# Attention with a gate: Q of the second half in seven block products, weights read back as stored parts

## The chip, the cores and the metric

The kernel runs on one core of a Trainium2 chip. The metric is the device time of one execution in microseconds. A core has TensorE (PE: matrix products into PSUM), VectorE (DVE), ScalarE (ACT), GpSimd (POOL) and SyncE (SP), which here only issues transfers; 16 DMA engines move data between DRAM and SBUF.

## What is computed

```python
def _A_ref(x, k_cache, v_cache, wq, wo):          # x: 1 x 2048 x 640, 32 heads of 128
    W = min(4096, max(256, Sk // 4))              # 512 keys, the last of 2048
    q = (x @ wq).reshape(B, Sq, Hq, Dh)           # by head
    scores = einsum("bhqd,bhkd->bhqk", q, k[last W]) * Dh ** -0.5
    p = softmax(scores)
    o = einsum("bhqk,bhkd->bhqd", p, v[last W])
    return o.reshape(B, Sq, Hq * Dh) @ wo
def _B_ref(x, w1, b1, w2, b2):
    return relu(x @ w1 + b1) ** 2 @ w2 + b2       # 640 -> 1728 -> 640
xn = layernorm(x)
return x + _A_ref(xn, ...) * silu(_B_ref(xn, ...))
```

## The kernel before

**Precision.** Each matrix product of float32 values is made of parts: an operand is split into a high part (a copy to float32r on ScalarE) and a low part (the value less its high part, on GpSimd or VectorE). `triple` issues three products, high·high, high·low and low·high, into one PSUM bank. One such product, 128 x 128 weights against 512 columns, is called a pass below.

**Stages.** The normalised x is transposed and split tile by tile (four tiles of 512 rows, `xT_d[t][i]` in DRAM, i = 0 high, 1 low). The dense branch B comes first; for its two middle tiles it already uses block products with seven multiplications (`w_first` to `w_third`). Then come 128 attention units.

**Units.** A unit is one head against one tile of 512 query rows. There are two halves (hf = 0: tiles 0 and 1; hf = 1: tiles 2 and 3), in each 16 groups of two heads (`G` = 2), in a group two tiles by two heads: four units (`UPG`). The last unit of the first half and the first of the second meet at the seam, unit 64. In a unit i TensorE makes:

- `s_mm`: scores of the unit, four banks s, 12 passes;
- `q_mm`: Q of unit i + 2 (`AHEAD`), bank pq, five blocks of D, 15 passes;
- `v_mm`: P·V of unit i - 1, bank o, 12 passes;
- `r_mm`: output products of a finished pair of heads, banks r, five blocks d in two units, 15 passes a unit on average.

The other engines work behind them. VectorE folds each score bank to a maximum (`max_fold`, tile rdm), ScalarE gathers it to 32 partitions (`gather`), VectorE ends it (`row`, rowm). SP stores that row to DRAM (m_d) and reads it back as a broadcast over 128 partitions (bm). VectorE subtracts it from the scores (`shift`, tile e), ScalarE takes the exponential (`expo`) and the high part of P (`p_hi`, pt), GpSimd the two low parts (`p_lo`) and between them the sum of the halves (`s_add`, su). The sum goes the same way over `s_fold`, `gather`, `row` (s_d) and a broadcast bs, with which VectorE scales o (`o_norm`); ScalarE and VectorE split it (`o_hi`, `o_lo`, ot), and `r_acc` adds each r to the accumulator acc.

Weights (`load_raw`, `prep`): in both halves the raw K, V, output and Q weights of each head are loaded (kr, vr, or, qr) and split into wk, wv, wo, wq.

**Order.** Nothing is scheduled by a tool: `at(when, f, ...)` collects calls with a planned time, sorted at the end, and each engine takes its instructions in that order. `PERIOD` = 12.4 is the planned length of a unit. `pe.addr_align` (rows ISA) pads TensorE's instruction stream so that units start at fixed slots.

Of the kernel before, what the change touches and what calls it, by code (L numbers as in the profile page):

```python
# [20 lines left out]
SLOTS = (0, 11, 22, 33, 42)  # L21
LEAD_SLOT, MID_SLOT, LEAD_PADS, LEAD_STEPS = 76, 101, 5, range(4, 21)
# [3 lines left out]
def kernel(  # L26
# [64 lines left out]
    s_d = [dpool.tile([P, DC, NT], F32, name=f"s_d{t}") for t in range(NTILE // 2)]  # L91
    h_d = {f: dpool.tile([P, NT], F32, name=f"h_d{f}") for f in range(FC - 4, FC)}
# [20 lines left out]
    W_HOME = {}  # L113

    def home(f, k):

        n = chunks[f][1]
        if (f, k) not in W_HOME:
            if k:
                w = [pc.tile([P, D], F32R, tag=f"w2{i}", name=f"w2s{f}_{i}", bufs=3) for i in range(2)]  # L120
            elif n < P:
                w = [xp.tile([P, DC, 2 * n], F32R, tag="w1h", name=f"w1s{f}", bufs=1)]
            elif f < FA:
                w = [
                    pa.tile([P, DC, n], F32R, tag=f"w1{i}", name=f"w1s{f}_{i}", bufs=3)
                    for i in range(2)
                ]
            else:
                two = keep.tile([P, 2, D], F32R, tag="ot", name=f"w1s{f}", bufs=4)
                w = [two[:, i, :].rearrange("p (c n) -> p c n", n=n) for i in range(2)]  # L130
# [258 lines left out]
    def split_hi(f, r, k):  # L389
        act.activation(split_parts(f, k)[0], r, AF.Copy)  # L390

    def split_lo(f, r, k, engine):
        hi, lo = split_parts(f, k)
        engine.tensor_tensor(lo, r, raw(hi), op=ALU.subtract)
# [454 lines left out]
    def pair(tag, shape, name, bufs):  # L849
        return [  # L850
            pools["eo" if tag == "wo" else "ep"].tile(shape, F32R, tag=f"{tag}{i}", name=f"{name}_{i}", bufs=bufs)
            for i in range(2)
        ]

    def load_raw(kind, hf, h):
        r = raw_tile(kind, f"{kind}r{hf}_{h}")
# [6 lines left out]
    def prep(kind, hf, h, eng=None):  # L863
        shape = {"q": [P, DC, DH], "k": [P, W], "v": [P, KC, DH], "o": [P, D]}[kind]
        home = {"q": WQ, "k": KT, "v": VV, "o": WO}[kind]
        hi, lo = home[hf, h] = pair(f"w{kind}", shape, f"w{kind}{hf}_{h}", 2 * G if kind == "o" else G)
        src = RAW.pop((kind, hf, h))
        act.activation(hi, src, AF.Copy)
        (eng or pool).tensor_tensor(lo, src, raw(hi), op=ALU.subtract)

# [89 lines left out]
    def s_add(i):  # L960
        RD[i, "su"] = ap.tile([P, 2, NT], F32, tag="su", name=f"su{i}", bufs=1)
        pool.tensor_tensor(RD[i, "su"], E[i, 0], E[i, 1], op=ALU.add)

    def s_fold(i):
# [3 lines left out]
            RD.pop((i, "su")).rearrange("p c (b i) -> p c b i", i=B32),  # L968
# [24 lines left out]
    def o_hi(i):  # L993
        two = keep.tile([P, 2, D], F32R, tag="ot", name=f"ot{i}", bufs=2 * G)
        OT[i] = [two[:, k, :NT] for k in range(2)]
# [5 lines left out]
    def r_mm(i, d, js, k):  # L1001
        hf, g, t, h = units[i]
        if 0 in js:
            PRS[i, d] = bank(f"r{i}_{d}", k)
        for j in js:
# [3 lines left out]
                tuple(x[:, d * P : (d + 1) * P] for x in w),  # L1009
# [21 lines left out]
    def load_finish(n, hf, t, d):  # L1031
        t0 = (hf * TPH + t) * NT
        FX[n, hf, t, d] = tile = raw_tile(n, f"f{n}{hf}_{t}_{d}")
# [24 lines left out]
    def late_load(kind, f):  # L1058
        f0, n = chunks[f]
        if f % 2 == 0 or kind == 1 and f == 3:  # L1060
            r = raw_tile("q" if kind == 1 else "o", f"l{kind}r{f}")
        elif kind == 1 and f == 1:
            r = raw_tile("o", f"l{kind}r{f}")
        else:
            tag, bufs = ("su", 1) if kind == 1 else ("e", 3)
            r = ap.tile([P, 2, NT], F32, tag=tag, name=f"l{kind}r{f}", bufs=bufs)
# [9 lines left out]
    def late_prep(kind, f):  # L1076
# [8 lines left out]
        else:  # L1085
            hi, lo = LW[kind, f] = pair("wo", [P, D], f"l2w{f}", 2 * G)
# [52 lines left out]
    def late_h():  # L1139
        LR["h"] = pools["ep"].tile([P, DC, NT], F32, tag="x1", name="lh", bufs=TPH)  # L1140
        for f in range(FA, FC):
            sp.dma_start(LR["h"][:, f - FA, :], h_d[f])

    def late_hs(f):
        two = ap.tile([P, 2, NT], F32R, tag=f"pt{f % 2}", name=f"lh{f}", bufs=3)
        hi, lo = LH[f] = [two[:, k, :] for k in range(2)]
        r = LR["h"][:, f - FA, :]
# [18 lines left out]
    def late_split(f):  # L1166
        n = chunks[f][1]
        r = LR.pop(f)
        kind, bufs = ("wk", G) if f % 2 else ("q", AHEAD + 1)
        if n < P:  # L1170
            h = pools["ep"].tile([P, NT], F32R, tag=f"{kind}0", name=f"lh{f}", bufs=bufs)
            LH[f] = (h, h)
            hi, lo = h[:n, :], h[n : 2 * n, :]
        else:
            hi, lo = LH[f] = pair(kind, [P, NT], f"lh{f}", bufs)
# [20 lines left out]
    def late_x():  # L1196
        LR["x"] = pools["ep"].tile([P, DC, NT], F32, tag="x0", name="lx", bufs=TPH)
        for d in range(DC):
            sp.dma_start(LR["x"][:, d, :], xT[d * P : (d + 1) * P, LATE * NT : (LATE + 1) * NT])

    def late_gate(d):
# [6 lines left out]
        for j in js:  # L1208
            dve.tensor_tensor(a[:, j], sg[:, j], a[:, j], op=ALU.mult)
            dve.tensor_tensor(a[:, j], a[:, j], LR["x"][:, d, j], op=ALU.add)  # L1210
# [64 lines left out]
    for m in range(2 * FC):  # L1275
# [44 lines left out]
    gate(  # L1320
        T2,
        lambda d: pools["ep"].tile([P, NT], F32, tag=f"wv{d % 2}", name=f"sgl{d}", bufs=G),
    )
# [6 lines left out]
    pools["eo"] = ctx.enter_context(tc.tile_pool(name="eo", bufs=1, side="right"))  # L1330
    ap = ctx.enter_context(tc.tile_pool(name="at", bufs=2))
# [10 lines left out]

    for n in range(HALF * NG):
        hf, g = divmod(n, NG)
        base = UPG * PERIOD * n
        for j in range(G):
            h = g * G + j
            for kind, when in (
                ("q", (j - 1 - AHEAD) * PERIOD + (8.42 if j else 8.35)),
                ("k", (j - 2) * PERIOD + (8.5 if j else 8.37)),  # L1350
                ("v", j * PERIOD + 8.4),
                ("o", (j if n == 0 else -j) * PERIOD + 8.45),
# [228 lines left out]
```

## Time and profile before

| | |
|---|---|
| median of 3 runs | 1956.58 us (1956.53 to 1957.04) |
| profiled execution | 1955.08 us, span 1953.3 us |
| granted TensorE clock | 0.999 |
| TensorE, VectorE, ScalarE, GpSimd busy | 99%, 82%, 64%, 69% of the span |
| matrix products | 8576 |
| Q blocks of attention | from 296.93 us on |

A row of the chain or of a timeline has the start in us, the length in us, the engine, the source line (here always a helper's), the operation, out<-in by the tiles' names, and in brackets the idle time ahead of it and who ended it. A row of groups has count, busy us, mean ns, and idle time with who ended it. Tile names without numbers stand for all units.

### The profile page before, as it was taken

The numbers are of one execution on the slowest core, as the hardware profiler recorded it, in microseconds if no ns is written. First come the engines' busy times: TensorE is split into PE (matmuls) and PEld (weight loads), VectorE is DVE, ScalarE is ACT, GpSimd is POOL, SyncE is SP. The second block draws the span as 40 slices with busy tenths as digits, with TensorE's granted clock in tenths as the row PEclk, the third lists the DMA queues.
The fourth block names the chain that finished last, engine by engine and source line by source line (L and its number), as shares of the span: only waits on it lengthen the run. The fifth ranks groups of instructions, "written<-read, shape, count | busy, mean of one in ns | idle before, by whom it ended". The sixth has DMA issues, their size and how long they took to land.

```text
span 1953.3 us, 28587 instructions
## 1 busy us (share of the span) xinstructions
PE 1943.1 (99%) x8576; PEld 1605.8 (82%) x8576; DVE 1599.5 (82%) x2758; ACT 1242.6 (64%) x2150; POOL 1348.2 (69%) x729
## 2 busy tenths in 40 slices
PE   9999999999999999999999999999999999999998
PEld 7888878888888888888888888888888888888887
DVE  6864747788888888888888878888888888888864
ACT  5665536766666666666666676666666666666643
POOL 1022106888888888888888888888888888888841
PEclk9999999999999999999999999999999999999999
DMA  7557953333332233333335433443343333323253
GB/s 267 150 179 252 365 176 112 98 93 92 93 92 93 92 93 92 93 93 92 92 98 179 144 110 109 114 114 114 114 114 114 114 114 114 98 92 93 85 186 119
DMA packets 147639, 246.43 MB, mean 126 GB/s; under 512 B 25020, under 2 KB 47334, under 8 KB 146214
## 3 DMA queue, kind: packets, MB, share of 16 engines
q1 hardware_dynamic: 144486, 230.02, 38.6%
q0 software_dynamic: 2864, 14.42, 1.8%
q8 instruction: 77, 1.26, 0.2%
q14 instruction: 68, 0.56, 0.1%
q10 hardware_dynamic: 144, 0.16, 0.0%
HBM read 213.59 MB, written 30.95 MB: 125 GB/s over the span
## 4 chain that ended last, share of the span: by engine, by line
PE 97%; DMA 2%; DVE 0%; issue 0%; ACT 0%; SPq 0%; ACTq 0%; POOLq 0%; DVEq 0%
PE r L77 22%; PE pq L77 22%; PE s L77 18%; PE o L77 18%; PE py L77 6%; PE ph L77 2%; PE ly L77 2%; PE wa L77 2%; PE lu L77 2%; PE wy L77 1%; PE wx L77 1%; DMA w1r<-in_w_dram 1%; DMA ch<-h_m 1%; PE eu L77 1%; DMA xb<-in_x_dram 0%; DMA w2r<-in_w_dram 0%
## 5 line engine op out<-in xcount | busy, mean ns | idle before, releaser
L77 POOL TENSOR_TENSOR pt<-e,pt 128x1024 fp32r<-128x1024 f32 x256 | 615.6, 2405 | 113.1 <-ACT pt L77 69.5
L77 PE MATMUL r<-ot,wo 128*128 128x512 f32 x1920 | 496.6, 389 | 0.0
L77 PE MATMUL pq<-ax,wq 128*128 128x512 f32 x1920 | 456.1, 389 | 0.0
L77 PEld LDWEIGHTS pq<-ax,wq 128*128 128x128 f32 x1920 | 360.4, 188 | 75.2 <-DVE q L77 0.4
L77 PEld LDWEIGHTS r<-ot,wo 128*128 128x128 f32 x1920 | 360.5, 188 | 74.7
L77 PE MATMUL s<-q,wk 128*128 128x512 f32 x1536 | 369.1, 389 | 1.4 <-DVE sgl L77 1.4
L77 PE MATMUL o<-pt,wv 128*128 128x512 f32 x1536 | 368.9, 389 | 0.0
L77 DVE TRANSPOSE_TENSOR_REDUCE rdm<-s 128x16 f32<-128x512 f32 x512 | 347.0, 712 | 6.3 <-PE s L77 5.3
L77 ACT ACTIVATE e<-e 128x1024 f32<-128x1024 f32 x256 | 269.8, 1054 | 123.1 <-DVE e L77 80.9
L77 PEld LDWEIGHTS s<-q,wk 128*128 128x128 f32 x1536 | 288.3, 188 | 61.5 <-DVE sgl L77 1.8
L77 PEld LDWEIGHTS o<-pt,wv 128*128 128x128 f32 x1536 | 288.4, 188 | 59.8
L77 DVE TENSOR_TENSOR e<-s,bm 128x512 f32<-128x512 f32 x512 | 312.6, 666 | 4.7 <-DMA bm<-m_d 4.1
L77 POOL TENSOR_TENSOR su<-e,e 128x1024 f32<-128x1024 f32 x128 | 309.1, 2415 | 0.0
L77 ACT ACTIVATE pt<-e 128x1024 fp32r<-128x1024 f32 x256 | 271.9, 1062 | 6.9
L77 ACT ACTIVATE rdm<-rdm 32x64 f32<-32x64 f32 x384 | 97.8, 255 | 183.5 <-DVE rdm L77 180.4
L77 DVE TENSOR_TENSOR acc<-r,acc 128x512 f32<-128x512 f32 x300 | 203.7, 679 | 12.9 <-PE r L77 12.5
L77 DVE TENSOR_TENSOR ot<-o,ot 128x512 fp32r<-128x512 f32 x128 | 88.5, 692 | 86.1 <-ACT ot L77 86.1
L77 DVE TRANSPOSE_TENSOR_REDUCE rds<-su 128x32 f32<-128x1024 f32 x128 | 158.3, 1237 | 0.2 <-POOL su L77 0.2
L77 ACT ACTIVATE q<-pq 128x512 fp32r<-128x512 f32 x128 | 76.7, 600 | 111.5 <-PE pq L77 111.5
L77 ACT ACTIVATE rds<-rds 32x32 f32<-32x32 f32 x384 | 89.7, 234 | 59.9 <-DVE rds L77 56.6
L77 POOL TENSOR_TENSOR wo<-or,wo 128x640 fp32r<-128x640 f32 x64 | 101.1, 1580 | 30.1 <-ACT wo L77 30.1
L77 POOL TENSOR_TENSOR wv<-vr,wv 128x512 fp32r<-128x512 f32 x64 | 83.3, 1301 | 52.1 <-ACT wv L77 45.3
(171 smaller groups left out, 2008.0 us busy)
## 6 DMA issues: line engine op xcount, KB each, us to landing
bm<-m_d SPq DMA_DIRECT2D x128, 256.0 KB, 3.2
bs<-s_d SPq DMA_DIRECT2D x128, 256.0 KB, 4.1
qr<-in_wq_dram SPq DMA_DIRECT2D x64, 320.0 KB, 4.3
or<-in_wo_dram SPq DMA_DIRECT2D x64, 320.0 KB, 4.7
kr<-in_kT_dram SPq DMA_DIRECT2D x64, 256.0 KB, 4.7
vr<-in_v_dram SPq DMA_DIRECT2D x64, 256.0 KB, 4.4
cw<-in_w_dram SPq DMA_DIRECT2D x26, 320.0 KB, 4.5
xT_d<-xT POOLq DMA_DIRECT2D x6, 1280.0 KB, 9.2
```

The lines of the kernel that those rows point to most:

```text
L77: ins = method(*args, **kwargs)
```

## The change

1. **Q of the second half.** For a pair of tiles (2 and 3) and a pair of heads, Q is a 2 x 2 block product (x blocks a11 to a22, each two blocks of D) made with seven products P1 to P7 of sums of x blocks (s1 to s4) and sums of Q weights (wta to wtd); the fifth block of D, which has no partner, is added by four plain products (r11, r12, r21, r22). The products accumulate in one bank: P1, copy out (u0), + P6, copy out (u1), + r22 and P7, copy out (u2), + P4 and r21: Q of one unit. Then P5 in a new bank, copied out (p5), which GpSimd adds to u1 and u2 (`z_add`). u0 is written back to the bank as a seed (c11) for P2 and r11; u1 as a seed (c12) for P3 and r12; u2 is the fourth Q.
2. **Sums of x.** s1 to s4 are made in the first half (`sum_load`, `sum_op`, `sum_high`, `sum_low`, `sum_store`; tiles a and sum), in even units from 2 to 56, and stored (sum_d). Around the seam high and low parts are loaded: high parts into the tiles of x, low parts into seven slots, some of them freed output weights and dense weights.
3. **Stored parts.** In the first half the split K, V and output weights are stored to DRAM (k_d, v_d, o_d) and in the second half loaded from there, K and V in one transfer of 512 KB, output weights in place in five pieces (`kv_load`, `wo_dma`).
4. **Places of transfers.** A1 to A4 (4.15 to 4.18) and B1 to B4 (8.55 to 8.58) of a unit, which is behind the issue of bm and of bs.
5. **Buffers.** e and pt have two buffers where they had three; `s_add` writes into e and su is gone.
6. **Order.** Units of the second half have 51 or 54 passes, three at the seam and three at the end 51 to 60; one more late up projection of B stands in the last units, where no Q is left.

```diff
+    SEAM = NU // 2
+    Q_END = NU - UPG
+    PASSES = {SEAM - 3: 60, SEAM - 2: 51, SEAM - 1: 60, NU - 3: 57, NU - 2: 51, NU - 1: 57}
+    for k in range(SEAM, Q_END + 1):
+        PASSES[k] = 51 + 3 * (k % 2)
...
+    A1, A2, A3, A4 = (4.15 + 0.01 * k for k in range(4))
+    B1, B2, B3, B4 = (8.55 + 0.01 * k for k in range(4))
...
+    ROWS = (
+        "s s s s r0 P3 v0 r1 r2 v1",
+        "s s s s r3 P1 v0 r4 P6 v1 r0",
+        "s s s s r1 P7 v0 r2 P4 v1",
+        "s s s s R21 r3 v0 P5 r4 P2 v1",
+    )
+    ROW = {k: ROWS[k % 4] for k in range(SEAM, Q_END + 1)}
...
+    def product(n, what, fresh=False):
+        x, w, c = PRODUCT[what]
+        for q in range(2):
+            triple(
+                BK[n],
+                [v[:, c + q, :] for v in WT[n, w]],
+                (AH[x][:, q, :], LOW[x][:, q, :]),
+                fresh and q == 0,
+                q == 1,
+                skip_group_check=True,
+            )
+    def copy_out(n, k, name):
+        act.activation(zt(k, f"{name}{n}"), BK[n], AF.Copy)
+    def seed(n, k, name):
+        new_bank(n, name)
+        act.activation(BK[n], ZT[k], AF.Copy)
+    def q_from(i, n, k):
+        QPS[i] = BK[n] if k is None else ZT[k]
+        q_hi(i)
+    def z_add(k, j):
+        pool.tensor_tensor(ZT[k], ZT[k], ZT[j], op=ALU.add)
...
+    def sum_op(k, a, b, op):
+        dve.tensor_tensor(ZT[k], ZT[a], ZT[b], op=op)
...
+        copies = T(u - 1, 7.95) if n == NG else done["P5"] + 0.1
+        at(copies, copy_out, n, 3, "p5_")
+        at(copies + 0.02, seed, n, 0, "c11_")
+        at(T(u, 3.2), q_from, u + 1, n, 2)
+        at(T(u, 4.05), q_lo, u + 1)
...
+    def kv_dma(kind, hf, h):
+        t = raw(KV[kind, hf, h]).rearrange("p i n -> p (i n)")
+        if hf == 0:
+            return sp.dma_start(split_d[kind, h], t)
+        sp.dma_start(t, split_d[kind, h])
...
-            E[i, k] = ap.tile([P, 2, NT], F32, tag="e", name=f"e{i}_{k}", bufs=3)
+            E[i, k] = ap.tile([P, 2, NT], F32, tag="e", name=f"e{i}_{k}", bufs=2)
...
-            ap.tile([P, 2, NT], F32R, tag=f"pt{n}", name=f"pt{i}_{k}_{n}", bufs=3)
+            ap.tile([P, 2, NT], F32R, tag=f"pt{n}", name=f"pt{i}_{k}_{n}", bufs=2)
...
-        RD[i, "su"] = ap.tile([P, 2, NT], F32, tag="su", name=f"su{i}", bufs=1)
-        pool.tensor_tensor(RD[i, "su"], E[i, 0], E[i, 1], op=ALU.add)
+        pool.tensor_tensor(E[i, 0], E[i, 0], E[i, 1], op=ALU.add)
```

In a line of ROWS s is one score bank (3 passes), r0 to r4 output products (6), v0 and v1 the two parts of P·V (6 each), P and R21 the products and the rest; P7, P2 and P3 have their rest with them (9 passes), R21 is 3.

TensorE in unit 99, second half, before: the end of the Q block of unit 101 (pq, weights wq), an output block (r95_4) and the first of P·V of unit 98.

```order
L77 MATMUL pq101_16381<-ax1_0_1_10908,wq1_19_0_16300 128x512
L77 MATMUL pq101_16381<-ax1_0_0_10907,wq1_19_1_16301 128x512
L77 MATMUL r95_4_16421<-ot94_15993,wo1_14_0_15477 128x512 x2
L77 MATMUL r95_4_16421<-ot94_15993,wo1_14_1_15478 128x512
L77 MATMUL r95_4_16421<-ot95_16132,wo1_15_0_15335 128x512 x2
L77 MATMUL r95_4_16421<-ot95_16132,wo1_15_1_15336 128x512
L77 MATMUL o98_16449<-pt98_0_0_16351,wv1_16_0_16021 128x512
```

In the same unit now: the end of P5 of group 25, the same output block, and the product P2 into the seeded bank c11.

```order
L78 MATMUL P525_16610<-ax1_0_1_11364,wtc25_0_16509 128x512
L78 MATMUL P525_16610<-wo1_2985,wtc25_0_16509 128x512
L78 MATMUL P525_16610<-ax1_0_1_11364,wtc25_1_16510 128x512
L78 MATMUL r95_4_16620<-ot94_16198,wo0_2984 128x512 x3
L78 MATMUL r95_4_16620<-ot95_16330,wo0_2984 128x512 x3
L78 MATMUL c11_25_16629<-ax1_1_0_11077,wtc25_0_16509 128x512
L78 MATMUL c11_25_16629<-ax1_1_1_11078,wtc25_0_16509 128x512
```

Six passes stand between the end of P5 and the first use of its bank as c11; P·V of unit 98 has been cut in two, with its first part ahead of these rows.

SP's issues in units 99 to 101 before: rows and broadcasts of the maximum (m_d, bm) and of the sum (s_d, bs), raw weights behind bs.

```order
L77 DMA m_d100_16532<-rowm100_16530 32x16
L77 DMA bm100_16534<-m_d100_16532 128x512
L77 DMA s_d99_16583<-rows99_16579 16x32
L77 DMA bs99_16585<-s_d99_16583 128x512
L77 DMA qr1_20_16597<-in_wq_dram 128x640
L77 DMA vr1_19_16599<-in_v_dram 128x512
```

And now, with stored parts of V (512 KB) and of output weights behind bm.

```order
L78 DMA m_d100_16733<-rowm100_16731 32x16
L78 DMA bm100_16735<-m_d100_16733 128x512
L78 DMA wv1_18_16746<-v_d18_137 128x1024
L78 DMA wo0_2984<-o_d8_159 128x512
L78 DMA s_d99_16782<-rows99_16778 16x32
L78 DMA bs99_16784<-s_d99_16782 128x512
```

The large transfers moved from behind bs to behind bm, between the broadcast and the row of the sum.

VectorE in unit 96 before, from the last fold of the scores to the sum's reduction.

```order
L77 TENSOR_REDUCE rdm96_15948<-s96_3_15959 128x16
L77 TENSOR_REDUCE rowm96_15981<-rdm96_15948 32x16
L77 TENSOR_TENSOR acc1_0_12100<-r93_1_15965,acc1_0_12100 128x512
L77 TENSOR_TENSOR o94_15900<-o94_15900,bs94_15898 128x512
L77 TENSOR_TENSOR ot94_15993<-o94_15900,ot94_15993 128x512
L77 TENSOR_REDUCE rds95_16002<-su95_15973 128x2x16
```

And now, where a Q low part made from the copied-out tile u2 stands ahead of rowm.

```order
L78 TENSOR_REDUCE rdm96_16141<-s96_3_16152 128x16
L78 SCALAR_TENSOR_TENSOR q97_1_16169<-u2_24_15930,q97_0_16168 128x512
L78 TENSOR_REDUCE rowm96_16179<-rdm96_16141 32x16
L78 TENSOR_TENSOR o94_16048<-o94_16048,bs94_16088 128x512
L78 TENSOR_TENSOR acc1_0_12335<-r93_0_16160,acc1_0_12335 128x512
L78 TENSOR_TENSOR ot94_16198<-o94_16048,ot94_16198 128x512
L78 TENSOR_REDUCE rds95_16207<-e95_0_16109 128x2x16
```

The accumulation moved in between o and ot, and the Q low part in between the fold and rowm.

More of the change, by code (lines that the diff above doesn't have):

```diff
@@ L1341, in at, with T @@
         plan.append((max(when, 0.0), len(plan), f, a))
+    SEAM = NU // 2
[3 more added lines that the diff above has]
+        PASSES[k] = 51 + 3 * (k % 2)
+    PASS = PERIOD / 54
+    START = [0.0]
+    for k in range(NU):
+        START.append(START[-1] + PASS * PASSES.get(k, 54))
+    def T(k, when=0.0):
+        if k < 0:
+            return k * PERIOD + when
+        return START[min(k, NU)] + max(k - NU, 0) * PERIOD + when
```

551 lines of the change are left out of this document (446 added, 105 removed).

## The prediction

> **What bounds the kernel now.** I read the page first, then the chain of waits in order of time, then the engines' shares by stretch.
>
> ```profile
> span 1953.3 us, 28587 instructions
> L77 PE MATMUL pq<-ax,wq 128*128 128x512 f32 x1920 | 456.1, 389 | 0.0
> 493.13 3.40 PE pq L77 x15
> ...
> 1007.21 3.40 PE pq L77 x15
> 500.00:990.00 490.00, 490.00 (x2163) 405.90 (x2162) 431.30 (x742) 322.43 (x561) 399.19 (x202) 1.00 0.31 92
> 1300.00:1790.00 490.00, 490.00 (x2164) 405.86 (x2163) 432.09 (x749) 322.36 (x560) 409.11 (x210) 1.00 0.36 109
> ```
>
> The two long rows give busy time of TensorE, weight loads, VectorE, ScalarE and GpSimd. TensorE is busy 490 of 490 us in both halves of attention at a granted clock of 1.00, and nothing idles ahead of the Q group. A Q block is 15 passes in 3.40 us: a pass is 0.2267 us (the 389 ns of the row overlaps its neighbours). Between the two quoted Q blocks lie 42 units in 514.08 us: 12.24 us each, exactly 54 passes. So a pass taken off TensorE in attention is taken off the time, until another chain is late. Two engines are near: VectorE has 432.09/490 of a unit, 10.79 us, and GpSimd 409.11/490, 10.22 us.
>
> **What goes.** In the second half a group of four units had 4 x 15 = 60 passes for Q; it gets seven products of 6 and four rests of 3, 54. Sixteen groups: 96 passes, 96 x 0.2267 = **21.8 us**. Scores, P·V, output and dense passes stay the same in number; one late up projection moves from the tail into the last units and is paid there. Units become 51 and 54 passes, 11.56 and 12.24 us, mean 11.90. With no new wait the profiled execution, 1955.1 us (span plus 1.8), would be 1933.3; the median of the runs shown lies 1.5 above it, and would be 1934.8.
>
> VectorE keeps its work per unit: 10.79 of 11.90, 91%. GpSimd loses the low parts of four kinds of weights, and gains sums and low parts of Q weights and two additions.
>
> ```profile
> L77 POOL TENSOR_TENSOR pt<-e,pt 128x1024 fp32r<-128x1024 f32 x256 | 615.6, 2405 | 113.1 <-ACT pt L77 69.5 <-POOL wv L77 22.4 <-POOL wk L77 14.4
> L77 POOL TENSOR_TENSOR wv<-vr,wv 128x512 fp32r<-128x512 f32 x64 | 83.3, 1301 | 52.1 <-ACT wv L77 45.3 <-issue 6.8
> ```
>
> These two give 0.20 us and 2.16 ns a column. Per group: eight low parts of P and four sums at 2.4 (28.9), two additions at 1.3, five weight sums (1152 columns, 3.5), eight weight low parts (2304 columns, 6.6): 41.6 us of 47.6, 87%. By load both fit, and ScalarE, with less to do than either, too. What is left is when things arrive.
>
> **P in time for V.** P·V starts at pass 21 to 27 of a unit now, at 37 before.
>
> ```profile
> 1504.81 2.88 PE L77 MATMUL s<-q,wk 128*128 128x512 f32 x12
> 1514.67 2.43 DVE L77 TENSOR_TENSOR e<-s,bm 128x512 f32<-128x512 f32 x4
> 1519.18 2.40 POOL L77 TENSOR_TENSOR pt<-e,pt 128x1024 fp32r<-128x1024 f32 x1
> 1523.89 2.42 POOL L77 TENSOR_TENSOR pt<-e,pt 128x1024 fp32r<-128x1024 f32 x1
> ```
>
> Counted from its scores, this unit subtracts at +9.86 and has its two low parts of P at +16.8 and +21.5. Some 1.0 of that is a finishing addition ahead of them on GpSimd, which in the tightest new unit doesn't stand there. P·V at pass 21 behind a 51-pass unit reads the first low part at 11.56 + 22 x 0.2267 = +16.55, against +15.8 to 16.0: 0.5 to spare. The second part of P·V moves back, to pass 42 or later: +21.3 at the tightest, against +20.5 to 21.3. E has two buffers for three, so the next subtraction now waits for that second low part; it is due at 11.56 + 9.86 = +21.4, just behind it. I cost these at nothing; if GpSimd is late by more, TensorE waits as long.
>
> **The new wait on TensorE.** Between P5 and P2 lie six passes, 1.36 us, in which ScalarE must copy P5 out and write the seed c11 into the same bank.
>
> ```profile
> 1511.61 1.52 PE L77 MATMUL r<-ot,wo 128*128 128x512 f32 x6
> 1511.81 0.60 ACT L77 ACTIVATE q<-pq 128x512 fp32r<-128x512 f32 x1 [0.81 <-PE pq L77]
> ```
>
> ScalarE starts 0.20 after TensorE went on to the next group; two copies at 0.60 and two handovers make 1.42 to 1.55. That is 0.05 to 0.2 of a wait per group. I take 0.1, **1.6 us** in 16 groups (0.8 to 3); behind it stand the second part of P·V and the next scores, which move with it.
>
> **VectorE and GpSimd at once.** The change adds VectorE instructions with both inputs in SBUF: 24 sums and low parts of x in the first half, and a Q low part per group (16) that comes from a copied-out tile, no longer from PSUM.
>
> ```profile
> 1861.38 2.41 POOL L77 TENSOR_TENSOR pt<-e,pt 128x1024 fp32r<-128x1024 f32 x1 [3.05 <-ACT pt L77]
> 1861.80 2.54 DVE L77 TENSOR_TENSOR lh<-lr,lh 128x512 fp32r<-128x512 f32 x1 [0.95 <-ACT lh L77]
> 1863.74 2.87 POOL L77 TENSOR_TENSOR su<-e,e 128x1024 f32<-128x1024 f32 x1
> L77 DVE TENSOR_TENSOR lh<-lr,lh x10: 684/758/2542, 1855.8 to 1922.8; 128x512 fp32r<-128x512 f32 x9, 64x512 fp32r<-64x512 f32 x1
> ```
>
> Such an instruction, 0.68 alone, took 2.54 when it met a GpSimd instruction: it ended 0.55 behind the end of that one, and the next one on GpSimd took 2.87 for 2.41. So each costs 0 to 1.9 us on VectorE and up to 0.5 on GpSimd. The Trainium skill (SBUF — State Buffer, Who interferes with whom) has this as a rule: with two SBUF inputs VectorE contends with a GpSimd instruction that reads SBUF, and the one that comes second blocks. By that rule alone the change is taxed 40 times; the trace agrees on the blocking, and tells how much of it is covered:
>
> ```profile
> 710.67 2.40 POOL L77 TENSOR_TENSOR pt<-e,pt 128x1024 fp32r<-128x1024 f32 x1 [1.24 <-issue]
> 710.09 2.76 DVE L77 TRANSPOSE_TENSOR_REDUCE rdm<-s 128x16 f32<-128x512 f32 x4
> 713.70 0.41 DVE L77 TENSOR_REDUCE rowm<-rdm 32x16 f32<-32x256 f32 x1 [0.85 <-ACT rdm L77]
> ```
>
> All of them are put between the folds (end 712.85) and rowm, where VectorE waits 0.85 for ScalarE in the even units that they stand in. GpSimd's low part ends 0.22 later, so 0.22 + 0.6 is covered: nothing in the first half. In the second half GpSimd's phase moves by some tenths, and I take 0.1 per group, **1.5 us** (0 to 16 x 1.7).
>
> **The broadcast of the maximum.** Behind rowm stand two transfers in series, the row to DRAM and bm back, and the large transfers are now issued right behind bm and bs.
>
> ```profile
> 703.30 0.33 SPq L77 DMA_DIRECT2D bm<-m_d  x1
> 706.77 2.43 DVE L77 TENSOR_TENSOR e<-s,bm 128x512 f32<-128x512 f32 x4
> 714.13 0.33 SPq L77 DMA_DIRECT2D m_d<-rowm  x1
> 715.50 0.33 SPq L77 DMA_DIRECT2D bm<-m_d  x1
> 719.32 2.43 DVE L77 TENSOR_TENSOR e<-s,bm 128x512 f32<-128x512 f32 x4
> DMA to landing us min/median/max: 3.0/3.2/3.3
> DMA to landing us min/median/max: 3.7/3.8/4.2
> bm<-m_d SPq DMA_DIRECT2D x5, 256.0 KB, 3.4
> bs<-s_d SPq DMA_DIRECT2D x6, 256.0 KB, 4.8
> ax<-xT_d SPq DMA_DIRECT2D x20, 256.0 KB, 2.9
> DVE e L77 <- DMA bm<-m_d: 1.0, 3, 0.5
> ```
>
> The first landing row is bm's in the first half, with nothing behind it; the second is bs's, with two loads 0.4 us behind. The last four are from the seam (1010 to 1080 us), where pieces of x (ax) of 256 KB follow bm: 3.4, and VectorE waited 1.0 us in all, which TensorE did not feel. With 512 to 768 KB behind it I expect bm at 3.4 to 4.1. VectorE comes to the subtraction 3.47 after the issue of bm in the first of the two units shown and 3.82 in the second, and recovers about 0.5 a unit before the next folds (0.33 of it because the folds, 2.76, wait for their scores, and take 2.43 when late). So up to about 4.1 it costs nothing; beyond that TensorE loses the excess in every unit. The Trainium skill (DMA: Bandwidth & Descriptors, Queues, rings and completion order) says that each DMA engine consumes descriptors in ring order: by that alone a follower would cost bm nothing. The rows disagree by 0.2 to 0.6 us, and go into the sum.
>
> At the seam 17 transfers of 512 KB and four of 256, 9.7 MB, are loaded where 20 of 256, 5.1 MB, were; up to 2.5 MB fall in one unit, so bm will be late there a few times: 0 to 5 us once, I take **1.5**.
>
> Sum: 1956.6 - 21.8 + 1.6 + 1.5 + 1.5 = **1939.4**.
>
> **Rivals.**
> 1. VectorE's loop in the second half.
>
> ```profile
> 701.46 0.41 DVE L77 TENSOR_REDUCE rowm<-rdm 32x16 f32<-32x256 f32 x1 [0.20 <-ACT rdm L77]
> 703.14 0.69 DVE L77 TENSOR_TENSOR ot<-o,ot 128x512 fp32r<-128x512 f32 x1 [0.67 <-ACT ot L77]
> ```
>
> Busy time 10.79, and in each unit 0.20 or 0.85 for the gather and 0.67 for the output part that ScalarE ends: 11.7 to 12.3 if nothing is put into these gaps. The new order puts accumulations and Q low parts there, which speaks against it; 91% speaks for it. If the mean unit stays at 12.1, 0.2 x 60 = 12 us of the gain are lost: 1947 (1944 to 1952).
> 2. The shared port in the second half, by the rule above: the Q low part meets the start of a GpSimd instruction, waits 1.9, and with the 0.85 of cover and 0.5 of slack leaves about 0.5 to 1 a group, in that and in P's chain: 8 to 16 us, 1948 to 1955.
> 3. **Slower:** bm behind the large transfers. If it lands at 4.8, as bs did at the seam, 0.7 us are missing in some 60 first-half units, which had no passes taken away: 1939 + 42 = 1981. It decides from 4.1; the 17 us of gain are eaten at 4.1 + 17/60 = 4.4. For it: bs. Against it: 3.4 with one follower, and stores that read SBUF and not DRAM.
> That the passes don't go, or go where TensorE waits anyway, is excluded by the order of TensorE's instructions and by 490 of 490.
>
> **How the numbers follow.** A change under 0.2% (3.9 us) can't be told from none here. Forecast 0.66 (1934.5 to 1944), rival 1 0.14, rival 2 0.07, rival 3 0.13. The range leaves out rival 3 and the worst of rival 2: 1934 to 1952. Faster than 1952.7: 0.66 + 0.14 + 0.04 = 0.84; within 0.2%: 0.04; slower: 0.12.
>
> **What would show it.** 8480 matmuls; units of 11.56 and 12.24 us in the second half; 12.24 still in the first; waits of TensorE almost only at c11, on ScalarE; bm landing at 3.4 to 4.1; the Q low part from u2 under 1.3 us. It is wrong if first-half units are longer than 12.24, if e waits for bm in most units, or if second-half groups take over 48.5 us.

## The result, and the profile after

| | before | after |
|---|---|---|
| median | 1956.55 us (1955.61 to 1957.04) | 2083.65 us (2077.08 to 2084.89) |
| ratio | | 1.0643, 95% interval 1.0621 to 1.0666 |
| span of the profiled execution | 1953.3 us | 2081.3 us |

The change makes the kernel 127 us slower; forecast were 17 us less. First the page of the changed kernel: its span, the chain that ended last by group, the scores and the subtraction with their idle time (the last column), and three of its transfers (count, KB, median us to landing).

```profile
span 2081.3 us, 29804 instructions
DMA bm<-m_d 7%; DMA m_d<-rowm 5%; PE s L78 4%; PE r L78 3%; DVE e L78 3%; POOL pt L78 3%; PE o L78 2%; PE ly L78 2%; ACT e L78 2%; DVE rdm L78 2%; PE P L78 2%; PE lu L78 1%; POOL e L78 1%; ACT pt L78 1%; DVE rowm L78 1%
L78 PE MATMUL s<-q,wk 128*128 128x512 f32 x1536 | 394.2, 406 | 82.0 <-DVE e L78 64.3
L78 DVE TENSOR_TENSOR e<-s,bm 128x512 f32<-128x512 f32 x512 | 318.0, 681 | 126.4 <-DMA bm<-m_d 107.5
bm<-m_d SPq DMA_DIRECT2D x128, 256.0 KB, 3.6
k_d<-wk SPq DMA_DIRECT2D x32, 512.0 KB, 4.3
wk<-k_d SPq DMA_DIRECT2D x32, 512.0 KB, 5.1
```

The scores wait 64.3 us for VectorE's subtraction, and that waits 107.5 us for the broadcast maximum. The chain that ended last runs for 12% of the span through two transfers in series: the row of the maximum to DRAM (m_d) and the broadcast back (bm). The stretches shown of before (first and last row), and the seam between them:

```profile
500.00:990.00 490.00, 483.88 (x2094) 389.63 (x2093) 422.67 (x735) 313.18 (x549) 393.43 (x194) 1.00 0.51 169
1000.00:1300.00 300.00, 256.96 (x1066) 201.51 (x1065) 210.16 (x361) 170.10 (x315) 202.66 (x126) 0.95 0.52 157
1300.00:1790.00 490.00, 458.31 (x1933) 364.74 (x1932) 402.26 (x692) 309.51 (x570) 388.70 (x258) 0.98 0.46 138
```

TensorE does 2094 passes in the first stretch where it did 2163, and 1933 in the last where it did 2164. For each unit I took the time from its first score product to that of the next, less its passes at 0.2267 us; the rest is what TensorE stood still. Summed (us):

| units | before | after |
|---|---|---|
| 0 to 60, first half | 0.5 | 29.9 |
| 61 to 68, seam | 0 | 30.7 |
| 69 | 0 | 16.8 |
| 70 to 124, second half | 0 | 71.2 |

Together 148.1 more; less the 21.8 us of passes that did go, that is 126.3 of the 128.0 by which the span grew. In the second half 59.6 of the 71.2 us stand ahead of the scores; in the first 12.9 of the 29.9 do, and 16.2 stand ahead of P·V, which waits for P and through it for the same maximum. Where a unit loses its time is seen in SP's queue, here in units 31 and 32 of the first half (start, length of the issue, transfer; two rows of VectorE after it):

```profile
691.56 0.33 SPq L78 DMA_DIRECT2D bm<-m_d  x1
691.94 0.43 SPq L78 DMA_DIRECT2D k_d<-wk  x1
692.42 0.42 SPq L78 DMA_DIRECT2D o_d<-wo  x1
694.09 0.32 SPq L78 DMA_DIRECT2D s_d<-rows  x1
697.28 0.32 SPq L78 DMA_DIRECT2D bs<-s_d  x1
697.65 0.72 SPq L78 DMA_DIRECT2D vr<-in_v_dram  x1
698.46 0.38 SPq L78 DMA_DIRECT2D or<-in_wo_dram  x1
702.15 0.33 SPq L78 DMA_DIRECT2D m_d<-rowm  x1
704.88 0.33 SPq L78 DMA_DIRECT2D bm<-m_d  x1
...
701.73 0.40 DVE L78 TENSOR_REDUCE rowm<-rdm 32x16 f32<-32x256 f32 x1
708.36 2.48 DVE L78 TENSOR_TENSOR e<-s,bm 128x512 f32<-128x512 f32 x4 [0.96 <-DMA bm<-m_d]
```

bm is issued when m_d has landed. In a unit of before these two stand 1.37 us apart (714.13 and 715.50, shown in the prediction), here 2.73 (702.15 and 704.88). What stands ahead of m_d are raw weights, and they are late themselves: SP issues them behind bs, bs waits for s_d, and s_d took 3.19 us (694.09 to 697.28) because two large stores stood ahead of it. Over units 4 to 60 the distance from m_d to bm is over 1.8 us in 40 of 57 units (before: 3), over units 70 to 124 in 28 of 55 (before: 11), at the seam in all 8, up to 5.75.

What the row of 702.15 waited for is seen in the bytes moved between 701.5 and 705.0 us (40 slices of 0.0875 us):

```profile
GB/s 334 252 193 228 117 176 176 88 117 82 59 53 29 0 23 0 28 14 27 23 23 23 29 29 29 29 0 29 29 29 29 2 0 0 0 0 0 0 0 0
```

Towards the end 23 to 29 GB/s are one packet per slice. The trace's packets are of 2048 bytes, then eight of 2560 one after the other (the widths of raw V and raw output weights), so one DMA engine is still at the raw weights. Of the row's 32 packets of 64 bytes 30 start by 703.13; the last two start at 704.26, behind the last raw one, and bm is issued at 704.88. Ahead of this a packet of 16 KB on the instruction queue had taken 0.92 us from 701.43 on; on which engine the trace does not say. So a row can be late when little is moved: one engine of 16 is enough.

In the second half bm also lands later. Before and after, us 1300 to 1900:

```profile
DMA to landing us min/median/max: 3.0/3.2/3.3
DMA to landing us min/median/max: 3.7/4.1/4.5
```

The mean distance from m_d to bm grows there from 1.52 to 2.11 us, less than this landing; in units 4 to 60 it grows from 1.42 to 2.27, and the landing only from 3.2 to 3.5 in the median.

The hole in unit 69 is of another kind:

```profile
1206.24 1.93 PE L78 MATMUL o<-pt,wv 128*128 128x512 f32 x6
1208.01 1.53 PE L78 MATMUL r<-ot,wo 128*128 128x512 f32 x6
1225.61 4.56 PE L78 MATMUL s<-q,wk 128*128 128x512 f32 x12 [16.08 <-issue]
```

TensorE stands for 16.08 us and waits for nothing that the profile shows. The trace has 253 empty instructions (NOP) of TensorE between the last score bank of this unit and the next unit; in the units beside it there are 2 to 7.

### The profile page after: what moved, and what is told of

It reads as the page before. It is cut to its first block, busy times and chain, and to the rows that moved or that the text cites. A ratio compares the mean times of both kernels' runs of the same rounds, so it can differ in the third digit from the quotient of the medians.

```text
span 2081.3 us, 29804 instructions
## 1 busy us (share of the span) xinstructions
PE 1978.2 (95%) x8480; PEld 1587.1 (76%) x8480; DVE 1619.9 (78%) x2791; ACT 1264.4 (61%) x2258; POOL 1372.6 (66%) x836
## 5 line engine op out<-in xcount | busy, mean ns | idle before, releaser
L78 PE MATMUL s<-q,wk 128*128 128x512 f32 x1536 | 394.2, 406 | 82.0 <-DVE e L78 64.3
L78 DVE TENSOR_TENSOR e<-s,bm 128x512 f32<-128x512 f32 x512 | 318.0, 681 | 126.4 <-DMA bm<-m_d 107.5
L78 PE MATMUL o<-pt,wv 128*128 128x512 f32 x1536 | 393.2, 393 | 7.5 <-POOL pt L78 5.1
L78 DVE TRANSPOSE_TENSOR_REDUCE rdm<-s 128x16 f32<-128x512 f32 x512 | 328.1, 689 | 35.3 <-PE s L78 34.8
L78 POOL TENSOR_TENSOR e<-e,e 128x1024 f32<-128x1024 f32 x128 | 322.0, 2516 | 10.0
L78 PE MATMUL pq<-ax,wq 128*128 128x512 f32 x960 | 228.1, 389 | 0.0
L78 PEld LDWEIGHTS pq<-ax,wq 128*128 128x128 f32 x960 | 180.1, 188 | 37.8 <-DVE q L78 0.4
L78 DVE TRANSPOSE_TENSOR_REDUCE rds<-e 128x32 f32<-128x1024 f32 x128 | 158.6, 1239 | 4.3 <-POOL e L78 3.7
L78 ACT ACTIVATE ot<-o 128x512 fp32r<-128x512 f32 x128 | 76.6, 599 | 36.8 <-DVE o L78 35.4
L78 PE MATMUL py<-ch,cw 128*128 128x512 f32 x410 | 94.0, 390 | 1.1 <-ACT cw L78 1.0
L78 DVE TENSOR_TENSOR o<-o,bs 128x512 f32<-128x512 f32 x128 | 86.9, 679 | 6.0 <-DMA bs<-s_d 5.8
```

The costliest lines, as they stand in the source:

```text
L78: ins = method(*args, **kwargs)
```

## The experiments

Ten kernels; the table first (medians in us, stalls as above), without e6_dose, which was run once to look at its units (1972.35 us):

| run | median | ratio to before, 95% | units 0–60 | seam | 69 | 70–124 |
|---|---|---|---|---|---|---|
| the change | 2083.65 | 1.0643 (1.0621–1.0666) | 29.9 | 30.7 | 16.8 | 71.2 |
| e1_align | 2070.96 | 1.0577 (1.0560–1.0593) | 32.5 | 30.4 | 1.8 | 68.8 |
| e2_actq | 2097.66 | 1.0726 (1.0705–1.0746) | 39.2 | 31.1 | 1.9 | 89.1 |
| e3_nostore | 2042.65 | 1.0443 (1.0423–1.0464) | 2.8 | 20.9 | 0.6 | 81.4 |
| e4_actlate | 2036.51 | 1.0421 (1.0399–1.0444) | 20.6 | 20.7 | 0.5 | 55.6 |
| e5_noload | 1965.01 | 1.0048 (1.0033–1.0063) | 1.9 | 12.6 | 0.6 | 16.7 |
| e7_bsum | 1964.98 | 1.0038 (1.0023–1.0053) | 2.7 | 10.0 | 0.5 | 17.0 |
| e8_noacc | 1956.21 | 0.9997 (0.9988–1.0007) | 2.5 | 12.4 | 0.6 | 4.3 |
| e9_balance | 2036.95 | 1.0406 (1.0391–1.0422) | 27.5 | 30.8 | 1.7 | 43.7 |
| e10_balact | 2020.82 | 1.0323 (1.0305–1.0340) | 21.8 | 22.2 | 0.6 | 39.6 |

**The hole in unit 69 (e1_align).** TensorE's instruction stream is padded so that units start at slots 128 instructions apart. From the slot of the last score bank, 42, to the next unit's first there is room for 86 instructions; unit 69 has 87, so the padding ran on to the same slot of the next block of 256.

```diff
+TIGHT = (0, 11, 22, 33, 41)
...
+    def slots(i):
+        if i in (69,):
+            return TIGHT
...
```

> The changed kernel, with the start slot of the last score bank of unit 69 at 41 instead of 42, so that its 87 TensorE instructions fit before the next unit's slot; nothing else. Theory: the one hole of 16.8 us in unit 69, in which TensorE waits for nothing that the profile shows, is the padding of the instruction stream by a whole block of 256, because one instruction too many stood there. Then unit 69 takes 12.2 to 13 us for 29.0, all other units stay, and the time is 2083.7 - 16 = 2067 (2064 to 2071). Rival: the hole is a late transfer at the seam that shows no releaser; then unit 69 stays near 29 us and the time stays within 2080 to 2085.

2070.96 us, 12.7 less; unit 69 loses 1.8 us (some 1 more than expected), and no wait on "issue" stands in the waits of TensorE any more. The profile has 29548 instructions for 29804, 256 fewer. The theory holds. All runs on the changed kernel below have this edit.

**The stores left out (e3_nostore).**

```diff
         if hf == 0:
-            return sp.dma_start(split_d[kind, h], t)
-        sp.dma_start(t, split_d[kind, h])
+            return
+        sp.dma_start(t, xT_d[0][0][:, 0:2, :].rearrange("p i n -> p (i n)"))
...
```

> As e1_align, without the 144 stores of the split K, V and output weights in the first half (37.7 MB left out); the second half loads as many bytes at the same places, but out of the stored x, so its results are other numbers. Theory (the large transfers delay the two small ones ahead of the broadcast): the first-half stalls, 30 us over 61 units, fall to 4 to 10 (loads for the sums of x stay), the seam loses some 5 of 31, the second half keeps its 71; the time is 2067 - 27 = 2040 (2034 to 2048). Rival (two buffers of e and pt in place of three, or the sums on VectorE, make the first half slow): its stalls stay over 20 us and the time is 2055 to 2067.

2042.65 us. The first half loses 2.8 us for 32.5, with the sums of x and the two buffers of e and pt still in it: they cost next to nothing, the stores cost 30. The second half is not helped: it loses 81.4, which is 12.6 more than in e1_align, and bm lands at 4.4 there for 4.1 (medians). It loads as many bytes, but out of the stored x; why that costs more is not shown.

**The loads left out too (e5_noload).**

```diff
-        kv_home(kind, 1, h)
-        kv_dma(kind, 1, h)
+        (KT if kind == "k" else VV)[1, h] = (KT if kind == "k" else VV)[0, H - G + h % G]
...
```

> As e3_nostore, and the second half loads no K, V and output weights at all: it uses the two last heads of the first half for every head (96 loads of stored parts, 64 of 512 KB and 80 of 256 KB less one group, left out; the results are other numbers). The products, the places of all other instructions and the two buffers of e and pt stay. Theory (the loads delay the maximum): the second half's stalls, 81 us in e3_nostore, fall to 5 to 20, the seam's from 21 to 10 to 17, and the time is 2043 - 73 = 1970 (1955 to 1985). Rival (VectorE's or GpSimd's load with shorter units and two buffers, rivals 1 and 2 of the prediction): the second half's stalls stay over 40 us and the time over 2000.

1965.01 us. The second half goes from 81.4 to 16.7 us and the seam from 20.9 to 12.6. So 102 us of span (2065.0 in e1_align, 1963.1 here) hang on the stored parts being moved, and the rest of the change, without them, is still 0.5% slower than before. The two stretches of e5_noload:

```profile
500.00:990.00 490.00, 489.96 (x2162) 405.30 (x2161) 439.86 (x757) 325.50 (x566) 407.42 (x201) 1.00 0.34 106
1300.00:1790.00 490.00, 487.95 (x2104) 391.50 (x2103) 432.60 (x750) 336.12 (x622) 420.88 (x279) 1.00 0.25 74
```

The first half is as before (2162 passes). In the second TensorE looks busy and does 2104 passes where the kernel before did 2164: its waits are short (93 of over 0.05 us, 0.16 in the mean) and many are inside groups of products. By these gaps 6.4 of the 16.7 us stand ahead of scores, 4.9 ahead of P·V and 3.3 ahead of the seeded products c.

**What is left in the second half (e8_noacc).** VectorE in e5_noload, units 84 and 85, from one set of folds (rdm) to the next:

```profile
1382.15 2.49 DVE L79 TRANSPOSE_TENSOR_REDUCE rdm<-s 128x16 f32<-128x512 f32 x4
1384.70 1.01 DVE L79 SCALAR_TENSOR_TENSOR q<-u,q 128x512 fp32r<-128x512 f32 x1
1385.64 0.40 DVE L79 TENSOR_REDUCE rowm<-rdm 32x16 f32<-32x256 f32 x1
...
1390.05 0.27 DVE L79 TENSOR_REDUCE sq<-rds 32x16 f32<-32x128 f32 x1 [0.21 <-ACT rds L79]
...
1393.72 2.49 DVE L79 TRANSPOSE_TENSOR_REDUCE rdm<-s 128x16 f32<-128x512 f32 x4
```

From 1382.15 to 1393.72 are 11.57 us, the length of a unit of 51 passes, and VectorE waits 0.21 in it: it has no slack to catch up. That is so in the units whose number is a multiple of 4 (busy 11.11 of 11.57 us in the mean); in the other units of 51 passes it is busy 9.07 of 11.69. The edit takes the additions to acc from it:

```diff
-        else:
+        elif not (hf == 1 and i < NU - UPG):
             a = ACC[hf, t][:, d, :]
             dve.tensor_tensor(a, pr, a, op=ALU.add)
```

> As e5_noload, and the additions of output products to the accumulator on VectorE are left out in the second half (2.5 of 0.65 us a unit; the results are other numbers). Theory (without the transfers VectorE's loop is what is left in the second half: in e5_noload it is without a gap through the units of 51 passes): the second half's stalls, 16.7 us, fall to 1 to 6, and the time to 1950 to 1956. Rival (the stalls there are what is left of late maxima, m_d to bm at 2.4 to 3.1 in every fourth unit, or GpSimd): they stay over 10 us and the time over 1959.

1956.21 us; the second half's stalls fall from 16.7 to 4.3, of which 3.3 are ahead of c. The waits ahead of scores and of P·V are both gone, so the late P was VectorE's doing too, not GpSimd's. The rival of the late maxima is not ruled out, though: the edit took them away as well. m_d to bm is over 1.8 us in 14 of the 55 units of e5_noload, 11 of them numbered 4k+2, and in 3 here, none of them such. Of the 12.4 us that went, some 7 stood in the units 4k+2 and 4k+3, mostly in or right behind those with a late row; some 5 stood in the other two, next to VectorE's full units.

**The seam (e7_bsum).** In e5_noload unit 61 alone loses 7.2 us. VectorE and GpSimd there:

```profile
1041.64 0.43 DVE L79 TENSOR_TENSOR wta<-wr,wta 128x256 f32<-128x256 f32 x1
...
1044.99 2.10 DVE L79 TENSOR_TENSOR wtb<-wr 128x256 f32<-128x256 f32 x1
1047.01 2.61 DVE L79 TENSOR_TENSOR wtb<-wr,wta 128x256 f32<-128x256 f32 x1
1049.55 0.82 DVE L79 TENSOR_TENSOR db<-wr,wr 128x128 f32<-128x128 f32 x1
1050.29 0.40 DVE L79 TENSOR_REDUCE rowm<-rdm 32x16 f32<-32x256 f32 x1
...
1044.40 2.40 POOL L79 TENSOR_TENSOR e<-e,e 128x1024 f32<-128x1024 f32 x1
1046.75 2.59 POOL L79 TENSOR_TENSOR pt<-e,pt 128x1024 fp32r<-128x1024 f32 x1
```

Two sums of Q weights that take 0.43 alone take 2.10 and 2.61 and end 0.3 us behind the end of a GpSimd instruction (1047.09 behind 1046.80, 1049.62 behind 1049.34); rowm, behind them, is 5 us late. The Trainium skill (SBUF — State Buffer, Who interferes with whom) has the rule, two SBUF inputs on VectorE contend with GpSimd for one port; these rows agree.

```diff
-        eng = dve if n == NG else pool
+        eng = dve if n == NG and what == "a" else pool
...
-            ("b", T(u - 3, 4.05), T(u - 3, 8.0), T(u - 3, 10.3)) if first
+            ("b", T(u - 3, 8.34), T(u - 3, 8.36), T(u - 3, 10.3)) if first
```

> As e5_noload, with the sums of Q weights wtb and db of the first group (unit 61) made by GpSimd behind its low part of P, and no longer by VectorE ahead of rowm, where two of them took 2.10 and 2.61 us beside a GpSimd instruction for 0.42 alone. Theory (the shared port holds VectorE, and rowm with it): m_d of unit 61 is issued at +5 to +7 of the unit for +11.8, the 7.2 us of stall in unit 61 fall to 0.5 to 3, and the time falls by 4 to 7 us from 1965.0, to 1958 to 1961. Rival (unit 61 is late for the transfers of x that stand ahead of its maximum): the stall stays over 5 us and the time within 1963 to 1967.

m_d of unit 61 is issued at +6.83 of the unit for +11.78, and the unit's loss falls to 1.7 us as expected, but the time stays, 1964.98: unit 62 now loses 3.6 for 1.2, its bm 4.78 us behind its m_d. One wait went and the next one took its place, with three transfers of x ahead of that m_d. On the time the theory was wrong.

**Order in the queue, or bytes (e2_actq, e4_actlate).** All new large transfers are issued by ScalarE on its own queue:

```diff
         if hf == 0:
-            return sp.dma_start(split_d[kind, h], t)
-        sp.dma_start(t, split_d[kind, h])
+            return act.dma_start(split_d[kind, h], t)
+        act.dma_start(t, split_d[kind, h])
...
```

> As e1_align, and all new large transfers (stored parts of K, V and output weights, both ways; sums of x; the parts of x at the seam) are issued by ScalarE on its own queue, at the same places of the order; the maximum and the sum with their broadcasts, raw weights and finish loads stay with SP. Theory (order in one queue): the 2-KB row of the maximum stands behind large transfers in SP's ring. Then the time from the issue of m_d to that of bm falls from 1.3 to 5.8 us to 1.3 to 1.7 in nearly all units, the stalls of 30 us in the first half, 31 at the seam and 71 in the second half fall to about a quarter, and the time is about 1970 (1955 to 1990). Rival (bandwidth: the 16 engines are busy with the large transfers whichever queue they come from): m_d to bm stays over 2 us in most units that have 2 or more large transfers, and the time is over 2040. A second rival, ScalarE held up by waits of the transfers in its own order, would show as idle time of ScalarE ahead of its transfers and as a time over 2040 too.

2097.66 us, slower still, and not the test that it was meant to be: ScalarE reaches the transfers earlier than SP did. Its two issues and SP's next two:

```profile
682.80 0.33 ACTq L79 DMA_DIRECT2D v_d<-wv  x1
683.17 0.44 ACTq L79 DMA_DIRECT2D o_d<-wo  x1
...
683.90 0.33 SPq L79 DMA_DIRECT2D m_d<-rowm  x1
686.21 0.33 SPq L79 DMA_DIRECT2D bm<-m_d  x1
```

768 KB on another queue, issued 1.1 and 0.7 us ahead, still make it 2.31 us from m_d to bm, and 1.88 or more in all of units 4 to 60. So a separate queue does not let the row pass. The Trainium skill (DMA: Bandwidth & Descriptors, Queues, rings and completion order) says that a DMA's semaphore increment lands only after every earlier write of the same DMA engine, across its queues; this row agrees. e4_actlate moves the places behind ScalarE's copy of Q:

```diff
-    A1, A2, A3, A4 = (4.15 + 0.01 * k for k in range(4))
+    A1, A2, A3, A4 = (7.85 + 0.01 * k for k in range(4))
```

> As e2_actq, with the places A1 to A4 moved from 4.15 to 7.85 of a unit, which is behind ScalarE's copy of Q: in e2_actq ScalarE issued the large transfers at +4.2 to +4.9 of a unit, just ahead of m_d (+5.4), 2 to 4 us earlier than SP does in the changed kernel. Theory (what counts is which bytes are in flight when m_d is issued, and SP's order only pushes them there): with the transfers at +7 to +8 they are over before the next m_d, m_d to bm is 1.3 to 1.8 us in most first-half units, the first half stalls under 12 us (32 in e1_align), the second half under 40 (69), and the time is about 2010 (1985 to 2030). Rival (ScalarE is held up by issuing, or the engines are too full at any place): m_d to bm stays over 2 us in most units, and the time over 2060.

2036.51 us: 61 less than e2_actq by the place alone, and 34 less than e1_align. The direction is the theory's, the size is not: 20.6 and 55.6 us of stall stay. In the first half m_d to bm is over 1.8 in 18 of 57 units (40 in e1_align), and s_d is still held (2.43 us to bs in the median), and the raw loads with it. In the second half it is over 1.8 in only 17 of 55 (before: 11), but bm lands at 3.8 in the median and up to 5.7 (before: 3.2 and 3.3).

**The price by itself (e6_dose).** The kernel before with added stores:

```diff
+    for k in range(6):
+        DOSE[16 + k] = ((4.02, sp, "pt"),)
+        DOSE[26 + k] = ((4.02, act, "pt"),)
+        DOSE[36 + k] = ((4.02, sp, "e"), (4.03, sp, "pt"))
+        DOSE[46 + k] = ((4.15, sp, "pt"),)
+        DOSE[54 + k] = ((4.15, sp, "e"), (4.16, sp, "pt"))
+    def dose(i, q, what):
+        d = dpool.tile([P, 2, NT], F32, tag="dose", name=f"dose{i}_{what}", bufs=4)
+        q.dma_start(d, raw(PT[i - 1, 1][0]) if what == "pt" else E[i - 1, 1])
...
```

> The kernel before, with stores of finished P or e tiles (512 KB each, into a buffer that nobody reads) added in five bands of six units of the first half; the results stay. Units 16 to 21: one store on SP's queue just ahead of m_d. 26 to 31: the same one on ScalarE's queue. 36 to 41: two (1 MB) on SP ahead of m_d. 46 to 51: one on SP just behind the issue of bm. 54 to 59: two behind bm. Theory (one queue is served in order, so that the 2-KB row waits for what stands ahead): m_d to bm 1.33 us without a store, 2.5 to 4 with 512 KB ahead, 4.5 to 6.5 with 1 MB ahead, 1.4 to 2.4 with 512 KB on the other queue; 1.33 with stores behind bm, and bm's landing there 3.2 to 3.7 us. Units get longer only where m_d to bm is over about 1.8. Rival (a store behind bm is as bad, as the prediction's third rival has it): bm lands at 4.5 or later in the bands behind bm, and their units get longer by 0.5 us or more.

SP's queue with one store ahead of m_d, with one behind bm, and with two behind bm (the end of one unit and the next):

```profile
537.38 0.33 SPq L77 DMA_DIRECT2D dose_pt<-pt  x1
537.79 0.38 SPq L77 DMA_DIRECT2D m_d<-rowm  x1
540.13 0.32 SPq L77 DMA_DIRECT2D bm<-m_d  x1
...
904.17 0.33 SPq L77 DMA_DIRECT2D bm<-m_d  x1
904.59 0.39 SPq L77 DMA_DIRECT2D dose_pt<-pt  x1
908.08 0.32 SPq L77 DMA_DIRECT2D s_d<-rows  x1
909.41 0.32 SPq L77 DMA_DIRECT2D bs<-s_d  x1
...
993.91 0.32 SPq L77 DMA_DIRECT2D s_d<-rows  x1
996.52 0.33 SPq L77 DMA_DIRECT2D bs<-s_d  x1
996.90 0.43 SPq L77 DMA_DIRECT2D vr<-in_v_dram  x1
997.43 0.38 SPq L77 DMA_DIRECT2D or<-in_wo_dram  x1
1000.72 0.32 SPq L77 DMA_DIRECT2D m_d<-rowm  x1
1003.62 0.33 SPq L77 DMA_DIRECT2D bm<-m_d  x1
```

The landing of bm in the last two bands:

```profile
DMA to landing us min/median/max: 3.4/3.5/3.5
DMA to landing us min/median/max: 3.4/3.4/3.6
```

- Ahead of m_d: 2.34 us to bm, 1.0 more than without, less than the 2.5 to 4 expected. The units grow by 1.1 to 1.4, and part of that is SP itself, which waited with m_d behind it until the stored tile was ready (m_d at +7.1 of the unit for +4.9). In the band of two the first store went out 3 us earlier; in five units that gave 2.43 and no second dose, and in one, where two raw loads had been issued shortly ahead of it, 4.02.
- On ScalarE's queue the store came 0.65 us behind m_d, and so told nothing of a store ahead: 1.33 to 1.40, units of 12.24.
- 512 KB behind bm: free. s_d to bs is 1.33 to 1.52, bm lands at 3.4 to 3.5 (first landing row), every unit 12.24.
- 1 MB behind bm: bm itself still lands at 3.4 (second row). But s_d takes 2.61, bs and the raw weights start late, and the next m_d takes 2.90 (s_d 2.6 to 4.1 in all six units, the next m_d 1.37 to 1.93 in the others). This is the chain of the changed kernel, made in the kernel before by two stores; in six units it cost 0.5 us. All these stores stand in the first half; loads behind bm, as in the second half, were not dosed.

**New places (e9_balance, e10_balact).** Only K or V, 512 KB, stays behind bm; output weights and finish loads go behind bs. e10_balact puts K and V on ScalarE's queue besides.

```diff
-            o_at = [(u + 1 + d + (n == 0), A2) for d in range(DC)]
+            o_at = [(u + 1 + d + (n == 0), B1) for d in range(DC)]
...
-            for d, (k, when) in enumerate(((2, A2), (2, B1), (2, B2), (3, B3), (4, A2))):
+            for d, (k, when) in enumerate(((2, B1), (2, B2), (3, B1), (3, B2), (4, B1))):
...
```

> As e1_align, with the transfers placed anew in SP's one queue: behind the issue of bm stands only the 512 KB of K or V of a unit; pieces of output weights (both halves) and the finish loads go behind bs (fs, fg and fx one to two units later than now, the finishing addition one unit later). The bytes stay; the seam is left as it is. Theory (a store behind bm holds s_d, s_d holds bs, and the loads behind bs then stand ahead of the next m_d; 512 KB behind bm were free and 1 MB was not in e6_dose, and e3_nostore bears over 1 MB behind bs): s_d to bs is under 2 us in most units, m_d to bm under 1.7, the first half's stalls fall from 32 to 3 to 10, the second half's from 69 to 20 to 40 (17 are VectorE's loop), the time to 2000 (1985 to 2015). Rival (what counts is the sum of bytes, wherever they stand): the stalls move to other units, and the time stays over 2045.

> As e9_balance, and the 512 KB of K or V are issued by ScalarE on its own queue behind its copy of Q (place 7.85), as in e4_actlate. Theory (a second queue lets the 2-KB row of the sum pass the large transfer): s_d to bs falls by some 0.3 us against e9_balance in the second half, and the time is 5 to 20 us below e9_balance. Rival (in place, the queue does not matter; ScalarE's issue costs more): the time is within 5 us of e9_balance or above it.

e9_balance: 2036.95 us, 34 less than e1_align. The second half falls from 68.8 to 43.7, the first only from 32.5 to 27.5, against 3 to 10 expected: s_d to bs is 1.88 in its median, as hoped, but the pieces now stand ahead of the raw weights behind bs, and m_d to bm is over 1.8 in 37 of 57 units. There the rival was right: the bytes had only moved. e10_balact: 2020.82 us, 16 less than e9_balance, in the range that was expected, but not where: the second half gives 4 of it, with s_d to bs at 1.70 for 1.84 in the median; the first half gives 6 and the seam 9. Nor is the queue all that differs: the places A1 to A4 move too, and K of unit 82, for one, goes out at +6.33 of the unit for +7.85. It is the fastest version with nothing left out, and 3.2% slower than before. Since even e5_noload, which moves none of the stored parts, loses 0.5%, no placing of these transfers alone would beat the kernel before.

## Why the prediction was wrong

- **Passes, −21.8: right.** 8480 products; units without a wait take 11.56 and 12.24 us in the second half, and 12.24 in the first.
- **The failed step: the broadcast of the maximum.** It stood in the sum at nothing outside the seam. The prediction counted what stands behind bm and asked when bm lands, free up to about 4.1. It did not count what stands ahead of the two 2-KB rows. Between m_d and bm lay 1.37 us in the rows that it quoted, and it let that stand; the mean is 2.27 in the first half and 2.11 in the second. The sentence on SP's queue that was missing: a large store behind bm is ahead of s_d, and through bs it moves the raw loads ahead of the next m_d. bm's own landing was as forecast in the first half (3.5 in the median, for 3.4 to 4.1), and e6_dose shows that stores behind it cost it little; in the second half it stood at the upper end, 4.1 in the median and up to 4.5, so there it had a part. From e1_align to e5_noload the two together are 30 us in the first half, 18 at the seam and 52 in the second.
- **The rule that I cited, used at one end only.** Ring order (the Trainium skill, DMA: Bandwidth & Descriptors, Queues, rings and completion order) was read as "a follower costs bm nothing". It says as much of what stands ahead, and there it speaks against this change; 2.34 for 1.33 us in e6_dose agrees.
- **Rival 3 had the sign, but not the mechanism where it looked.** It put the loss in bm's own landing in the first half, at 4.8, from 4.1 on. bm never got there in the first half (3.7 at most); the loss was in the leg before it. More than half of the loss fell in the second half and the seam, where the rival had counted none, and there the landing did pass 4.1.
- **The seam, 1.5: mis-sized.** 30.7 measured: 10 go with the stores (e3_nostore), 8 with the loads of stored parts (e5_noload), and the 12.6 left I put down to the pieces of x and the weight sums of the first group; e7_bsum moved the loss between them and so did not size either. The sums I had put on GpSimd with all others; for the first group the code has them on VectorE, where beside GpSimd they took up to 2.6 us.
- **VectorE's loop, rival 1: right in size, and given too small a chance.** Without the stored parts' transfers 12.4 us go when VectorE is relieved (16.7 less 4.3), priced at 12; the sum would have been some 1952 us with it, not 1939. Some 5 of them stand next to its full units and some 7 mostly in or behind late rows, which went with the same edit. "91%" was the mean; VectorE is full in every fourth unit, where it waits 0.21 of 11.57 us.
- **The seed c11, 1.6: right in kind, half in size.** 3.3 us ahead of c in 14 groups (e5_noload), 0.24 a group for 0.1.
- **P for V, nothing: right for GpSimd, by e8_noacc.** The waits of P·V go when VectorE is relieved, and those of the first half, 16.2 us, go with the stores (1.6 in e3_nostore).
- **The shared port: covered in the first half, as argued** (2.8 us of stall in all with the sums there, e3_nostore). In the second the low part from u2 takes 1.01 for 0.66, within VectorE's loop: 0.35 a group for 0.1.
- **Unit 69 was not in the text.** A unit with one instruction too many cost 15.0 of the 16.8 us; the order of instructions could have been counted against the 128 of a unit.

What stays open: how the second half's loss (71.2 us, 16.7 in e5_noload) divides between the stored parts and the finish loads between which they stand, and between m_d to bm and the landing of bm; what the instruction packets add (of the 68 rows over 1.8 us outside the seam, 45 have one between 1.5 us ahead of their issue and 1.0 behind it; before it was 13 of 14, and TensorE did not stand still); and what e9_balance would give with the sums of x moved away from the units in which two output pieces stand. None of these was tried.

## What to carry to other kernels

For each small transfer on the critical path, write down what stands ahead of it in its queue, not only what follows it, and go round the loop once: a large transfer put behind one small one stands ahead of the next. Count bytes per unit against the room between two small transfers (512 KB behind bm was free, 1 MB was not) before trading engine work for memory traffic. When a mean share of 91% hides units of several kinds, make the sum for the fullest one.

## What the runs showed of the hardware

- A 2-KB row that lets the next transfer go 1.33 us after its issue takes 2.34 with 512 KB issued 0.4 us ahead on its queue, and 2.31 with 768 KB issued 1.1 and 0.7 us ahead on another one. What the second queue itself is worth is not shown, since e10_balact, 16 us faster than e9_balance, also changes the times of issue; the Trainium skill (DMA: Bandwidth & Descriptors, Issuing engines are not separate DMA queues) expects only the issue time to be saved by that.
- The DMA share was 0.46 to 0.52 where the rows were late: mean load says little of the delay of one small transfer. In unit 32 one engine of 16 held the row for 1.1 us.
- An overrun by one instruction in an aligned stream cost 15.0 us: 253 empty instructions, with no releaser in the profile.
- The granted clock was 0.95 and 0.98 in the two stretches in which TensorE stood still most, and 1.00 in the last one of e5_noload. The passes themselves were not slower by much: gaps of under 0.05 us make 2.6 of the 71.2 us of units 70 to 124.
